# Two attentions over 2048 positions on one core: the first 1024 positions' rows fetched behind the key differences, maxima 20 steps ahead instead of 22, and another order of the lead

## The chip, the core and the metric

The kernel runs on one core of one Trainium2 chip. The metric is the device time of one execution in microseconds (us). Three executions of the kernel before are the measure; one more was taken with the hardware profiler, and all lines of a profile below come from that one.

## What is computed

Two attentions over the same x (2048 positions, width 576, 32 heads of 18 columns) are mixed by a gate. A has its own keys and values for each head; in B all heads share one set of keys and values.

```python
g = _sigmoid((x * gate_w).sum(-1, keepdims=True))
a = _A_ref(x, A_wqkv, A_wo)      # softmax(q k^T * 18**-0.5) v, 32 heads, then @ wo
b = _B_ref(x, B_wq, B_wk, B_wv, B_wo)   # the same with one k and one v for all heads
return g * a + (1 - g) * b
```

All is float32, and the softmax must subtract each row's maximum: B's queries and keys are drawn eight times as large as A's.

## The kernel before, in words

There are 64 units, one for each head: units 0 to 31 are B's, 32 to 63 are A's. A unit has 16 steps, one for each 128 keys, so there are 1024 steps, and step T belongs to unit T // 16. A step makes the scores of 128 keys with all 2048 queries in four matmuls of 512 queries (`step_scores`, L757, "s" in the strings below), ScalarE takes the exponential of each (L765), and TensorE multiplies the results with the values (L772, the digits in the strings, in quarters of 128 columns).

A row's maximum must be known before its unit's first scores. It is found ahead, by a second pass of matmuls over the same product with queries and keys in each other's place: for a block M of 128 queries, the scores with 512 keys are made at L712 and VectorE reduces them (L721, "m"). A cheaper way takes two chunks of 512 keys at once: a matmul with the *difference* of two key chunks ("x", from the tile `kdb` or `keb`), of which ScalarE keeps the positive part (L715), and a matmul with the first chunk ("y"), to which VectorE adds that part and reduces (L718). So an "x" and a "y" do the work of two "m", with one VectorE reduction in place of two, and one ScalarE operation more. In the steady strings each pair of blocks (2p, 2p+1) takes an x, a y and six m. The maxima run LEAD = 22 steps ahead of the scores (L28).

When all 16 blocks of unit u are reduced, `max_rows(u)` (L723) makes a row of them: a last reduction and a transpose on VectorE (L728, L730), a split in two halves (L246, L248; on GpSimd from unit 2 on), a DMA to DRAM (`m_d<-mh`) and two DMAs back into two rows of the unit's query tile (`qs<-m_d`), which the scores' matmul subtracts as part of its product. It is called from the loop at L1258 where a string begins at T = 16u - 6.

Before the steady loop come two stages. In the first (to some 33 us) x is loaded and split into a high and a low part, and the first two weight tiles are multiplied with it in four chunks of 512 positions (`project`, L283). The rows that come out go through DRAM, since they must change partitions: `leave_first` writes q and k rows to `kq` and the key differences to `kd`, and `back`, `back2` and `load_kd` bring them back as `ksb`, `qs` and `kdb`. All but chunk 2's go on SyncE's queue; chunk 2's writes and its two reads go on GpSimd's (`late`). The second stage is the lead (`lead_steps`, L1148, to some 79 us): its string makes the first 24 blocks' maxima with x and y for both halves of the keys (`lead_max`, L1125: 47 x and 47 y; the matmuls are L1131, the reductions L1141, the positive parts L1135), and puts between them the halves A and B of six more weight units (`half_step`, L980). Blocks are taken as (0..7, first half of the keys), (8..15, first), (0..7, second), (8..15, second), (16..23, first), (16..23, second). After the 32nd y, unit 0 is complete and `max_rows(0)` is called (L1143). The string ends with the first eight scores, between fillers ("f", L1099).

The order of all matmuls is written in strings; a small clock (`Clock`) only picks which of seven PSUM banks each one takes. In the steady loop a string covers eight steps, the last 22 steps run scores alone, two at a time, with the last output units between them (L1275). `begin(T)` (L1185) issues what is due at step T and one step of the slow normalisation, except where T % 16 == 10.

SyncE's DMAs carry eight semaphores in turn: a DMA waits until the one eight places before it has landed, beside what its data need.

Of the kernel before, what the change touches and what calls it, by code (L numbers as in the profile page):

```python
# [27 lines left out]
LEAD = 22  # L28
# [133 lines left out]
def gated_mix_kernel(ctx: ExitStack, tc: tile.TileContext, xT, wall, wv, wo, out):  # L162
# [190 lines left out]
    def back(t, i, b, x0, x1, put=dma):  # L353
        n = 64 if i < 3 else 54
        put(t[b:b + n, x0:x1], kq_d[54 * i:54 * i + n, x0:x1])

    def back2(t, i, x0, x1, put=dma):
        for b in (SB, MB):
            back(t, i, b, x0, x1, put)

    def first_back():
        load_kd(kdb, ROW_KB)
        back2(qs[0], 1, 512, 1024)
# [17 lines left out]
    with tc.tile_pool(name="xs", bufs=1, side="right") as xsp:  # L381
# [90 lines left out]
        back(ksb, 0, SB, 0, 512)  # L472
        back2(qs[0], 1, 0, 512)
# [623 lines left out]
    def keep_busy():  # L1097
# [6 lines left out]
                   for M in range(M0, M0 + 8)][:-1]}  # L1104
# [43 lines left out]
    def lead_steps(ops):  # L1148

        for op in ops.replace(" ", ""):  # L1150
# [12 lines left out]
            else:  # L1163
# [5 lines left out]
    lead_steps("ABABABABABxABxyABABxyABABxyABABxyABABxyABABxyABABxyABABxyABA"  # L1169
               "BxyABABxyABABxyABABxyABABxyABABxyABABxyABABxyABvABxyABxyABvA"  # L1170
               "BxyABxyABvABxyABxyABvABxyABxyABABxyABxyABABxyABxyABABxyABxyA"
               "BABxyABxyABABxyABxyABABxyABxyABABxyABxyABABxyABxyABABxyABxyA"
               "BABxyABxyBBxyBxyBByBsfsfsfsfsfsfmsfms")
# [11 lines left out]
    def begin(T):  # L1185

        for f in at.get(T, []) + at.get(T + 1, []):
            f()
        if slow and T % 16 != 10:
            for _ in range(2 if T > 1000 or 914 < T < 930 else 1):  # L1190
                if slow:
                    try:
                        next(slow[0])
                    except StopIteration:
                        slow.pop(0)

    out_last = out_proj(8, [P])

    def emit(ops, units=0):
        for op in ops.replace(" ", ""):  # L1200
# [7 lines left out]
            elif op in "xy":  # L1208
# [4 lines left out]
                if op == "y":  # L1213
                    step_max(*divmod(2 * pos["y"], 16), 0)
                    pos["y"] += 1
            elif op == "m":
                M, c = plain.pop(0)
                step_max(*divmod(M, 16), c)
            elif op in "AB":
# [36 lines left out]
    while pos["s"] < 4 * (NSTEP - LEAD):  # L1256
        T = pos["s"] // 4
        if (T + LEAD) % 16 == 0 and (T + LEAD) // 16 - 1 < NU:  # L1258
            max_rows((T + LEAD) // 16 - 1, nc.gpsimd if T > 16 else nc.vector)
# [12 lines left out]
    max_rows(NU - 1)  # L1272


    emit("ssssss 8 ssssssUssss 7 ssssss 8 ssssss 9 ssssssUssss 7 ssssss 9 ssssssUsssss 7 ssss 6 ssssss 3 a 6 ssssssbUcssss 6 ssssssVVVVVVVVsssssss 9 9 2", 4)  # L1275
# [38 lines left out]
```

## Time and profile before

| | |
|---|---|
| median of 3 runs | 2639.48 us (2637.72 to 2640.01) |
| the profiled execution, by its own time | 2641.33 us |
| its span, first to last instruction | 2639.5 us |
| busy in the span: PE, ACT, DVE, POOL | 99%, 93%, 91%, 36% |
| first scores of unit 0 on PE | 78.62 us |
| 33.00 to 79.00 us: PE, DVE, ACT busy | 39.34, 34.94, 34.69 us of 46.00 |
| 79.00 to 2440.00 us: PE, ACT, DVE busy | 2361.00, 2236.38, 2201.30 us of 2361.00 |
| 2580.00 to 2600.00 us: ACT busy, DVE busy | 20.00, 2.85 us of 20.00 |

PE is TensorE, ACT ScalarE, DVE VectorE, POOL GpSimd and SPq SyncE's queue, where the length of a row is the time in which DMAs are issued, not that in which they move. In a row of the timeline the first number is the start, the second the length, and the bracket is the idle time before it, with what ended it. The ends of matmuls are modelled, so a PE at 99% is not a PE without waits. 1.83 us of the execution's own time lie outside its span.

### The profile page before, as it was taken

Reading aid. Unit: us, or ns where it says so; the run is one execution under the profiler, and the core shown is the slowest. Engines: PE = TensorE matmul, PEld = TensorE weight load, DVE = VectorE, ACT = ScalarE, POOL = GpSimd, SP = SyncE. Lnnn points to the kernel's source line nnn. Section 1 sums busy time; section 2 is a strip of 40 time slices with the busy share of each in tenths; the row PEclk is TensorE's granted clock in tenths of the full one; section 3 lists DMA queues with packets and bytes.
Section 4 is the critical chain, followed back from the end, with each engine's and each line's share of the span. In section 5 each row is a group of like instructions: output and inputs, shape, how many; then the busy total and the mean of one; then the engine's idle time right before and its main releaser. Section 6 shows DMA issues by size and latency. Waiting matters only on the chain.

```text
span 2639.5 us, 67524 instructions
## 1 busy us (share of the span) xinstructions
PE 2622.6 (99%) x25446; PEld 1416.8 (54%) x25446; DVE 2391.9 (91%) x4575; ACT 2450.5 (93%) x4864; POOL 942.5 (36%) x1192
## 2 busy tenths in 40 slices
PE   8999999999999999999999999999999999999999
PEld 6545545555555554554545545545455555545665
DVE  6999999999999999999999999999999989999883
ACT  5999999999999999999999999999999999999887
POOL 3345332211045435644555355544641020012113
PEclk9999999999999999999999999999999999999999
DMA  7332322212133324332544345444442333223312
GB/s 223 90 103 86 93 78 73 88 60 61 52 112 112 95 92 115 118 92 86 147 138 137 120 123 160 131 126 133 142 137 83 112 104 88 76 85 122 114 57 92
DMA packets 186305, 280.81 MB, mean 106 GB/s; under 512 B 59876, under 2 KB 147140, under 8 KB 174535
## 3 DMA queue, kind: packets, MB, share of 16 engines
q1 hardware_dynamic: 169931, 223.68, 29.5%
q0 software_dynamic: 15168, 51.43, 5.3%
q8 instruction: 200, 3.28, 0.5%
q10 hardware_dynamic: 880, 1.39, 0.1%
q14 instruction: 126, 1.03, 0.1%
HBM read 200.74 MB, written 66.90 MB: 101 GB/s over the span
## 4 chain that ended last, share of the span: by engine, by line
PE 97%; DVE 0%; POOL 0%; ACT 0%; issue 0%; ACTq 0%; DVEq 0%
PE acc L772 38%; PE bank L712 29%; PE bank L757 18%; PE bank L980 11%; PE acc L784 1%; PE bank L960 1%; PE bank L1131 0%; POOL oacc L953 0%; PE bank L1034 0%; DVE junk L1141 0%; PE bank L339 0%; DVE oacc L955 0%; ACT tmp L952 0%; ACT xd L1135 0%; PE acc L1099 0%
## 5 line engine op out<-in xcount | busy, mean ns | idle before, releaser
L765 ACT ACTIVATE pt<-bank 128x512 f32<-128x512 f32 x4096 | 2150.4, 614 | 127.9 <-PE bank L757 71.1
L721 DVE TENSOR_REDUCE mx<-bank 128x1 f32<-128x512 f32 x3002 | 1888.3, 684 | 128.6 <-PE bank L757 63.5
L757 PE MATMUL bank<-qs,ksb 56*128 56x512 f32 x2688 | 912.2, 424 | 0.0
L712 PE MATMUL bank<-ksb,qs 54*128 54x512 f32 x2270 | 815.6, 426 | 0.0
L772 PE MATMUL acc<-pt,vb 128*19 128x256 f32 (+3 forms) x6112 | 551.5, 457 | 0.0
L712 PEld LDWEIGHTS bank<-ksb,qs 54*128 54x128 f32 x2270 | 385.5, 184 | 292.0 <-ACT pt L765 159.0
L772 PE MATMUL acc<-pt,vg 128*19 128x512 f32 (+3 forms) x5952 | 531.5, 455 | 0.0
L757 PEld LDWEIGHTS bank<-qs,ksb 56*128 56x128 f32 x2688 | 442.8, 184 | 159.0 <-DVE mx L721 66.4
L757 PE MATMUL bank<-qs,ksa 56*128 56x512 f32 x1408 | 468.1, 425 | 0.0
L712 PE MATMUL bank<-ksa,qs 54*128 54x512 f32 x1232 | 441.0, 425 | 0.0
L718 DVE CUSTOM_DVE_ANT_0 junk<-bank,xb 128x512 bf16<-128x512 f32 x500 | 342.9, 686 | 34.2 <-PE bank L757 26.6
L715 ACT ACTIVATE xb<-bank 128x512 f32<-128x512 f32 x500 | 292.5, 604 | 17.1 <-PE bank L757 7.4
L712 PEld LDWEIGHTS bank<-ksa,qs 54*128 54x128 f32 x1232 | 209.8, 184 | 142.4 <-ACT pt L765 80.6
L757 PEld LDWEIGHTS bank<-qs,ksa 56*128 56x128 f32 x1408 | 225.8, 184 | 83.8 <-DVE mx L721 33.7
L246 POOL CAST rhl<-rst 128x292 fp32r<-128x292 f32 (+2 forms) x95 | 40.0, 421 | 579.6 <-issue 343.3
L772 PEld LDWEIGHTS acc<-pt,vb 128*19 128x19 f32 x6112 | 123.2, 97 | 212.7 <-issue 182.4
L772 PEld LDWEIGHTS acc<-pt,vg 128*19 128x19 f32 x5952 | 121.6, 97 | 212.0 <-issue 185.8
L246 POOL CAST mh<-mt 128x32 fp32r<-128x32 f32 x62 | 13.0, 210 | 561.3 <-DVE mt L730 453.2
L980 PE MATMUL bank<-xr,wrh 64*128 64x292 f32 (+1 forms) x1386 | 204.1, 300 | 0.0
L980 PEld LDWEIGHTS bank<-xr,wrh 64*128 64x128 f32 x1386 | 170.0, 186 | 3.5
L712 PE MATMUL bank<-kdb,qs 54*128 54x512 f32 x372 | 161.0, 433 | 0.0
L575 POOL TENSOR_TENSOR xr<-xst,xr 128x876 fp32r<-128x876 f32 (+1 forms) x77 | 159.2, 2068 | 0.0
(175 smaller groups left out, 2441.2 us busy)
## 6 DMA issues: line engine op xcount, KB each, us to landing
qs<-qk SPq DMA_DIRECT2D x366, 144.0 KB
xst<-xT SPq DMA_DIRECT2D x66, 438.0 KB
qk<-rhl POOLq DMA_DIRECT2D x66, 292.0 KB, 4.4
ksa<-qk SPq DMA_DIRECT2D x132, 144.0 KB
xst<-xT SPq DMA_DIRECT2D x66, 146.0 KB
xst<-xT SPq DMA_DIRECT2D x132, 73.0 KB
ksb<-qk SPq DMA_DIRECT2D x60, 144.0 KB
onh<-oh POOLq DMA_DIRECT2D x32, 256.0 KB, 3.6
```

Source lines behind the costliest of these rows:

```text
L246: eng_h.tensor_copy(h, src)
L575: nc.gpsimd.tensor_tensor(x[:, 5:8, 0:n], t0, x[:, 0:3, 0:n].bitcast(F32), op=OP.subtract)
L712: nc.tensor.matmul(pm, qs[u % 3][b:b + 54, i * P:(i + 1) * P], k, start=True, stop=True)
L715: nc.scalar.activation(MX["x", u, i], pm, AF.Relu)
L718: nc.vector.tensor_tensor_reduce(junk, pm, MX.pop(("x", u, i)), 1.0, -3e38, op0=OP.add, op1=OP.max, accum_out=MX[u][:, i, c:c + 1])
L721: nc.vector.tensor_reduce(MX[u][:, i, c:c + 1], pm, axis=AX.X, op=OP.max)
L757: nc.tensor.matmul(ps, kst(u)[b:b + 56, i * P:(i + 1) * P], qs[u % 3][b:b + 56, c * 512:(c + 1) * 512], start=True, stop=True)
L765: nc.scalar.activation(pt, ps, AF.Exp, scale=SCALE)
L772: nc.tensor.matmul(acc[32 * j:32 * j + 19, a:b], v_of(u, i), PT[u, i, j][:, a:b], start=(i == 0), stop=(i == 15), skip_group_check=True)
L784: nc.tensor.matmul(acc[32 * j:32 * j + 19, 256 * half + a:256 * half + b], v_of(NU - 1, i), pt[:, x + a:x + b], start=(i == 0), stop=(i == ...
L960: nc.tensor.matmul(fp[:, 0:u.n], x, y, start=(n == 0), stop=(n == len(u.ops) - 1))
L980: nc.tensor.matmul(u.fp[op][:, 0:u.n], x[b:b + 64], y[b:b + 64], start=(n == 0), stop=(n == last))
```

## The change

Five edits go together:

1. The reads of `ksb` and `qs` for the first 512 positions, which stood ahead of chunk 1's writes on SyncE's queue, now stand behind the read of `kdb`, and the four reads of `qs` become two of 1024 positions.
2. LEAD is 20: the lead makes 22 blocks' maxima (43 x and 43 y), and the steady loop takes over the two others.
3. The lead's string begins with nine pairs of A and B instead of five ahead of the first x; the rest is spread anew. It has as many A, B, v and f as before.
4. `max_rows(u)` is called as soon as the seventh operation of the unit's last pair is emitted, no longer at the start of a string.
5. Two more steps of the old tail get a pair of blocks beside their scores, and the tail is eight scores shorter. The slow steps leave out T % 16 == 12 instead of 10.

```diff
-LEAD = 22
+LEAD = 20
...
     def first_back():
         load_kd(kdb, ROW_KB)
-        back2(qs[0], 1, 512, 1024)
+        back(ksb, 0, SB, 0, 512)
+        back2(qs[0], 1, 0, 1024)
...
         high_x(4)
-        back(ksb, 0, SB, 0, 512)
-        back2(qs[0], 1, 0, 512)
         rows = leave_first(1, F0)
...
-    lead_steps("ABABABABABxABxyABABxyABABxyABABxyABABxyABABxyABABxyABABxyABA"
+    lead_steps("ABABABABABABABABABxABxyABABxyABABxyABABxyABABxyABABxyABABxyA"
...
-        if slow and T % 16 != 10:
+        if slow and T % 16 != 12:
...
+    def formed(p):
+
+        FORMED[p] = FORMED.get(p, 0) + 1
+        if FORMED[p] == 7 and p % 8 == 7:
+            max_rows(p // 8, nc.gpsimd if p > 15 else nc.vector)
...
                     pos["y"] += 1
+                    formed(pos["y"] - 1)
             elif op == "m":
                 M, c = plain.pop(0)
                 step_max(*divmod(M, 16), c)
+                formed(M // 2)
...
-    while pos["s"] < 4 * (NSTEP - LEAD):
+    while pos["s"] < 4 * (NSTEP - LEAD - 2):
         T = pos["s"] // 4
-        if (T + LEAD) % 16 == 0 and (T + LEAD) // 16 - 1 < NU:
-            max_rows((T + LEAD) // 16 - 1, nc.gpsimd if T > 16 else nc.vector)
...
-    max_rows(NU - 1)
+    emit("msmssm 4 smsmsmsys 4")
...
-    emit("ssssss 8 ssssssUssss 7 ssssss 8 ssssss 9 ssssssUssss 7 ssssss 9 ssssssUsssss 7 ssss 6 ssssss 3 a 6 ssssssbUcssss 6 ssssssVVVVVVVVsssssss 9 9 2", 4)
+    emit("ssssssUss 7 ssssss 8 ssssss 9 ssssssUssss 7 ssssss 9 ssssssUsssss 7 ssss 6 ssssss 3 a 6 ssssssbUcssss 6 ssssssVVVVVVVVsssssss 9 9 2", 4)
```

Three places show what moved. SyncE's queue at the end of the first stage, before (`phl` are projected rows, `pdhl` the key differences; the first four writes of `kq`, chunk 0's, stand just ahead of this):

```order
L168 DMA ksb<-kq 64x512
L168 DMA qs_90<-kq 64x512 x2
L168 DMA kq<-phl 54x2x512
L168 DMA kq<-phl 54x512
L168 DMA kd<-pdhl 18x1024
L168 DMA kd<-pdhl 18x512
L168 DMA kdb<-kd 54x512
L168 DMA qs_90<-kq 64x512 x2
```

and SyncE's queue at the same place in the changed kernel:

```order
L168 DMA kq<-phl 54x2x512
L168 DMA kq<-phl 54x512
L168 DMA kd<-pdhl 18x1024
L168 DMA kd<-pdhl 18x512
L168 DMA kdb<-kd 54x512
L168 DMA ksb<-kq 64x512
L168 DMA qs_90<-kq 64x1024 x2
```

The three reads that waited for chunk 0's writes have moved from ahead of chunk 1's writes to behind `kdb`.

TensorE around the first x of the lead, before, with the engines and DMA semaphores that a matmul waits for (`kdb` marks an x, `ksb` a y, `xh` and `xl` the halves of a weight unit):

```order
L980 MATMUL bank0_476<-xh_119,wl_180 128x512
L980 MATMUL bank1_478<-xh_119,wl_180 128x512
L1131 MATMUL bank2_488<-kdb_94,qs0_90 128x512 [waits DMAHW7_49,DMAHW4_49,PE_49]
L980 MATMUL bank0_476<-xh_119,wl_180 128x512
L980 MATMUL bank1_478<-xh_119,wl_180 128x512
L1131 MATMUL bank3_494<-kdb_94,qs0_90 128x512 [waits DVE_49]
L1131 MATMUL bank4_498<-ksb_93,qs0_90 128x512 [waits DMAHW5_49,DMAHW6_49,PE_49,Activation_49]
```

and TensorE around the first x in the changed kernel, whose line numbers are one lower:

```order
L979 MATMUL bank0_474<-xl_120,wh_179 128x512
L979 MATMUL bank1_476<-xl_120,wh_179 128x512
L1130 MATMUL bank2_494<-kdb_94,qs0_90 128x512 [waits DMAHW4_49,DMAHW1_49,PE_49]
L979 MATMUL bank0_474<-xl_120,wh_179 128x512
L979 MATMUL bank1_476<-xl_120,wh_179 128x512
L1130 MATMUL bank3_500<-kdb_94,qs0_90 128x512 [waits DVE_49]
L1130 MATMUL bank4_504<-ksb_93,qs0_90 128x512 [waits DMAHW2_49,DMAHW3_49,PE_49,Activation_49]
```

The first x stands four A-B pairs later, and waits for two DMAs as before, `kdb` and a read of `qs`; the second x takes, before and now, a bank that VectorE must have read (bank3, which held the projection `project(1, 1)`).

SyncE's queue at the first rows of the steady loop, before (`m_d_73` and `qs_91` are unit 1's row of maxima, `wrst` and `xst` the weights and x of the next weight units):

```order
L168 DMA m_d_73<-mh 128x64
L168 DMA qs_91<-m_d_73 1x64x32 x2
L168 DMA wrst<-wall 128x512
L168 DMA wrst<-wall 64x128 x2
L168 DMA xst<-xT 128x3x292
L168 DMA xst<-xT 128x292
```

and the same place of SyncE's queue in the changed kernel:

```order
L168 DMA xst<-xT 64x292 x2
L168 DMA wrst<-wall 128x512
L168 DMA wrst<-wall 64x128 x2
L168 DMA m_d_73<-mh 128x64
L168 DMA qs_91<-m_d_73 1x64x32 x2
L168 DMA qs_90<-qk 18x2048 x6
```

Unit 1's row has moved behind the loads that are due at step 10. Counted in scores emitted, the row of unit u is now called for between 3 and 4.25 steps ahead of its unit's first scores, where it was 6: 3 or 3.25 steps in units 1, 8, 17, 49 and 57 to 62, 3.75 to 4.25 in all others.

More of the change, by code (lines that the diff above doesn't have):

```diff
@@ L1103, in gated_mix_kernel @@
     pairs = {"x": [(M, h) for M0, h in ((0, 0), (8, 0), (0, 1), (8, 1), (16, 0), (16, 1))
-                   for M in range(M0, M0 + 8)][:-1]}
+                   for M in range(M0, min(M0 + 8, LEAD + 2))][:-1]}
     pairs["y"] = list(pairs["x"])
@@ L1168, in gated_mix_kernel @@
     begin_units(lead_units())
-    lead_steps("ABABABABABxABxyABABxyABABxyABABxyABABxyABABxyABABxyABABxyABA"
[L1170 to L1173, printed above, removed]
+    lead_steps("ABABABABABABABABABxABxyABABxyABABxyABABxyABABxyABABxyABABxyA"
+               "BABxyABABxyABABxyABABxyABABxyABABxyABABxyABABxyABABxyABvABxy"
+               "ABABxyABvABxyABABxyABvABxyABxyABvABxyABxyABABxyABxyABABxyABx"
+               "yABABxyABxyABABxyABxyABABxyABxyABABxyABxyABABxyABxyABABxyABx"
+               "yBBxyBxyBByBsfsfsfsfsfsfmsfms")
     clk.half = HALF_MM
@@ L1197, in gated_mix_kernel @@
     out_last = out_proj(8, [P])
+    FORMED = {}
+    def formed(p):
+        FORMED[p] = FORMED.get(p, 0) + 1
+        if FORMED[p] == 7 and p % 8 == 7:
+            max_rows(p // 8, nc.gpsimd if p > 15 else nc.vector)
     def emit(ops, units=0):
```

## The prediction

> **What bounds the kernel now.** I read the page first, then the timeline of TensorE for the lead.
>
> ```profile
> span 2639.5 us, 67524 instructions
> PE 2622.6 (99%) x25446; PEld 1416.8 (54%) x25446; DVE 2391.9 (91%) x4575; ACT 2450.5 (93%) x4864; POOL 942.5 (36%) x1192
> ```
>
> Three engines are above 90% over the whole span, so the steady loop leaves little to win, and its strings are not changed. What can be won lies where TensorE stands still, and the timeline of TensorE shows that at the start of the lead (L980: weight units; L1131 with `kdb`: an x).
>
> ```profile
> 33.18 1.20 PE L980 MATMUL bank<-xh,wh 64*128 64x512 f32 x8
> 34.22 0.39 PE L980 MATMUL bank<-xh,wl 64*128 64x512 f32 x2
> 39.28 0.76 PE L1131 MATMUL bank<-kdb,qs 54*128 54x512 f32 x1 [4.67 <-issue]
> ...
> 48.62 0.39 PE L1131 MATMUL bank<-kdb,qs 54*128 54x512 f32 x1
> ...
> 49.32 0.39 PE L1131 MATMUL bank<-kdb,qs 54*128 54x512 f32 x1
> ```
>
> TensorE stops for 4.67 us ahead of the first x, which waits for `kdb`. Counting the x from 0, number 8 starts at 48.62, and the next 0.70 later: that is the pace of the string there. The stretches right after the stop, with the granted clock after the five engines' busy times:
>
> ```profile
> 39.20:44.10 4.90, 4.82 (x22) 4.13 (x24) 1.86 (x5) 2.39 (x4) 0.57 (x2) 0.50 0.66 165
> 44.10:50.00 5.90, 4.77 (x37) 3.55 (x35) 4.50 (x14) 4.63 (x9) 2.94 (x3) 0.99 0.75 234
> ```
>
> After the stop TensorE runs 4.9 us at half its clock, which costs another 2.4 us. Why `kdb` comes so late stands on SyncE's queue.
>
> ```profile
> 16.68 5.16 SPq L168 DMA_DIRECT2D kq<-phl  x4
> 29.16 0.46 SPq L168 DMA_DIRECT2D ksb<-kq  x1
> 29.67 1.24 SPq L168 DMA_DIRECT2D qs<-kq  x2
> 31.01 0.82 SPq L168 DMA_DIRECT2D kq<-phl  x2
> 31.88 1.94 SPq L168 DMA_DIRECT2D kd<-pdhl  x2
> 35.53 0.27 SPq L168 DMA_DIRECT2D kdb<-kd  x1
> ```
>
> The read of `ksb` stands from 21.84 (16.68 + 5.16) to 29.16 until chunk 0's writes have landed, and the key differences wait behind it, though VectorE has them at 26.05:
>
> ```profile
> 25.37 0.68 DVE L315 TENSOR_TENSOR pdhl<-pd,pdhl 18x512 fp32r<-18x512 f32 x1
> ```
>
> **The reads behind `kdb`.** The writes of `kd` can now be issued from 26.05 and take 1.94 us, to 28.0; the read of `kdb` follows 1.71 us after that, as it did (35.53 against 31.88 + 1.94), so at 29.7, where it was 35.53. If the writes must queue behind chunk 0's, 29.16 is the least, and 31.5 I take as the most (chunk 0's writes themselves took 7.3 us from their last issue). Behind it come `ksb` (0.46) and two reads of `qs` (1.24, now of twice the bytes), so the last is issued from 31.3 on. `kdb` needed 3.75 us from issue to use (39.28 - 35.53); with that and up to 1 us for the double size the first x may start at 35.0 to 36.0. TensorE gets there at 33.18 + 9 x 0.26 = 35.5 (eight matmuls, four pairs, took 1.04 us). So the first wait goes. What is late next is the second x: its bank was read by VectorE's last operation ahead of the joins.
>
> ```profile
> 37.19 0.69 DVE L294 TENSOR_TENSOR phl<-bank,phl 128x512 fp32r<-128x512 f32 x1 [0.28 <-ACT phl L290]
> 41.07 0.69 DVE L1141 CUSTOM_DVE_ANT_0 junk<-bank,xd 128x512 bf16<-128x512 f32 x1 [3.19 <-DMA kq<-phl]
> ```
>
> It ends at 37.88. Nothing on VectorE ahead of it moves much, so x1 stands at some 37.8, and this covers a late `kdb` too: up to 31.5 costs nothing. With 0.70 for each x, x8 would be due at 37.8 + 7 x 0.70 = 42.7.
>
> But x8 needs block 8, the first of chunk 2, which goes over GpSimd's queue and is not moved; its writes wait for VectorE at 33.82. The reads, and from the view of DMAs their time to landing:
>
> ```profile
> 38.72 1.05 POOL L168 DMA_DIRECT2D qs<-kq  x2 [2.44 <-issue]
> qs<-kq POOLq DMA_DIRECT2D x2, 128.0 KB, 6.0
> kq<-phl POOLq DMA_DIRECT2D x1, 216.0 KB, 3.8
> ```
>
> The second read is issued at 39.25 and landed at 45.3; x8 came later than that anyway (48.62), so nothing shows it in the trace of before. In the changed kernel it ends a wait. Its bounds are 43.0 (with the 3.8 us of a larger write on the same queue) and 45.3; I take 43.5, since `kdb` and two reads of `qs`, which used the DMA engines from 35.5 on, are through by then. So x8 at 43.5 in place of 48.62, and the stop ahead of it is 0.8 us, too short to make TensorE slow again (a stop of 1.13 us at 47.81 lies in the stretch at 0.99).
>
> The Trainium skill (DMA: Bandwidth & Descriptors, Anatomy of one DMA) gives a DMA of GpSimd's queue 2.0 us and its bytes at 436 GB/s, an estimate of 2.3 us for 128 KB. The row says 6.0, so the trace disagrees; by that rule block 8 would be there at 41.6, x8 at 42.7, and the sum below 0.8 us better.
>
> From x8 to the 32nd y, which completes unit 0, and on to the first scores:
>
> ```profile
> 68.42 0.69 DVE L1141 CUSTOM_DVE_ANT_0 junk<-bank,xd 128x512 bf16<-128x512 f32 x1
> ...
> 69.15 0.22 DVE L728 TENSOR_REDUCE m<-mx 128x16 f32<-128x64 f32 x1
> 69.41 0.21 DVE L730 STREAM_TRANSPOSE mt<-m 128x32 f32<-128x32 f32 x1
> ```
>
> ```profile
> 70.31 0.35 SPq L168 DMA_DIRECT2D m_d<-mh  x1
> 73.74 1.31 SPq L168 DMA_DIRECT2D qs<-m_d  x2
> ```
>
> ```profile
> 78.62 0.39 PE L757 MATMUL bank<-qs,ksb 56*128 56x512 f32 x1
> ```
>
> From x8 it is 19.8 us to that y (68.42 - 48.62). The new string has 42 pairs of A and B there, the old one 40; two of 0.23 make it 20.3, so the y is at 63.8. Behind it stood 15 more joins at 0.61 (VectorE's pace in a row, below) and the row, 10.2 us in all to the first scores; four joins fewer make 7.8. The row's own way becomes the longer: its last read is issued until 75.05, 6.6 us after the y, and lands 1.4 to 3.1 us later (3.1 if it needs `kdb`'s 3.75 from its start), 8.0 to 9.7 in all; I take 8.3, since the rows are 8 KB. So the first scores come at 63.8 + 8.3 = 72.1 instead of 78.62: **-6.5 us**, between -7.6 and -3.3.
>
> **Lead 20 and the tail.** The two blocks that leave the lead are done beside two steps that ran scores alone.
>
> ```profile
> 2574.35 31.96 ACT L765 ACTIVATE pt<-bank 128x512 f32<-128x512 f32 x65 [0.42 <-PE bank L757]
> ```
>
> ScalarE runs the tail without a gap, 31.96 us for 65, so 0.49 each, and eight scores are 3.9 us. With blocks beside them, they take nine operations of ScalarE, 4.4 us, and six reductions and a join of VectorE, 6 x 0.61 + 0.69 = 4.35 us; at most the 4.8 us of two steady steps (14.3 us for six, 139.42 to 153.72 below). **+0.7 us**, 0.5 to 0.9. Output units, scores and values are as many as before.
>
> **The rows of maxima in the loop.** The row of unit u starts 1.75 to 3 steps later than before. Unit 2, then unit 58, whose way was the longest: the last reduction, GpSimd where it was busy, the two reads, the unit's first scores.
>
> ```profile
> 139.42 0.22 DVE L728 TENSOR_REDUCE m<-mx 128x16 f32<-128x64 f32 x1
> ```
>
> ```profile
> 141.98 1.25 SPq L168 DMA_DIRECT2D qs<-m_d  x2
> ```
>
> ```profile
> 153.72 0.39 PE L757 MATMUL bank<-qs,ksb 56*128 56x512 f32 x1
> ```
>
> ```profile
> 2355.80 0.22 DVE L728 TENSOR_REDUCE m<-mx 128x16 f32<-128x64 f32 x1
> ```
>
> ```profile
> 2358.76 1.28 POOL L867 TENSOR_TENSOR ot<-ot,R 128x512 f32<-128x512 f32 x1 [10.90 <-DMA R<-r_d]
> ```
>
> ```profile
> 2362.03 1.25 SPq L168 DMA_DIRECT2D qs<-m_d  x2
> ```
>
> ```profile
> 2370.10 0.50 PE L757 MATMUL bank<-qs,ksb 56*128 56x512 f32 x1
> ```
>
> From reduction to the end of the reads' issue it is 3.8 us in unit 2 and 7.5 in unit 58; with some 1.6 to land, 5.4 and 9.1. Six steps gave 14.3 us. Of 4.25 steps, 10.1 us, 1.2 go for the last matmul and join ahead of the reduction; 8.9 remain, over 3 more than usual. Of three steps, 7.15 us, 5.95 remain: just enough. Behind a late row wait the unit's scores and everything after them on TensorE. Most of the ten units with 3 or 3.25 steps should just make it; unit 58's delay came from a normalisation step that stood ahead of it on GpSimd, and which now stands three steps ahead. **+0.3 us**, 0 to 4. The reduction and transpose themselves (0.43) now stand two steps into a string. In a steady string VectorE looks so:
>
> ```profile
> 1016.99 6.08 DVE L721 TENSOR_REDUCE mx<-bank 128x1 f32<-128x512 f32 x10
> 1023.45 2.48 DVE L721 TENSOR_REDUCE mx<-bank 128x1 f32<-128x512 f32 x4 [0.38 <-PE bank L757]
> ```
>
> Ten reductions follow each other (0.61 each), and 0.38 us of idle time behind them take up the 0.43: nothing in the sum.
>
> **The sum.** -6.5 + 0.7 + 0.3 = -5.5 us. The profiled execution's own time is 2641.33 us, 1.83 outside its span; it would become 2635.8. It stands 1.85 us above the median of the runs, 2639.48, so the forecast for that is **2634.0 us**, 0.21% less. About 0.2%, or 5.3 us, is what a measurement of this kernel tells from no change.
>
> **Rivals.** *Chunk 2 holds the lead.* If the second read on GpSimd's queue lands at 45.3 as before, x8 stops 2.6 us and the gain falls to -3.7; if TensorE then goes to half its clock, as after the stop of 4.67 us, another 2.4 are lost. For it speaks the 6.0 us row, against it the smaller traffic. 2635.8 to 2638.2, say 2636.5: no change that can be told. Chance 0.23. The Trainium skill (TensorE: Matmul & The Clock Gate, Part 1) has the clock halve after an idle window of some 3.4 us; the 0.50 after 4.67 us agrees, and by that rule a stop of 2.6 us would mostly not do it.
>
> *VectorE's row reduction reaches TensorE.* If the 0.43 us in mid-string is not taken up and a fifth of it reaches TensorE in 62 units, 5.3 us go, and the time is 2639.3: no change. Against it stand the 0.38 us, for it that strings with two units have no such gap that I saw. Chance 0.15.
>
> *The rows come late.* With three steps, 5.95 us are left for a way of 5.4. If GpSimd or SyncE's queue holds those ten rows as it held unit 58's, up to 3.2 us are lost in each. From 1.1 us each the kernel is slower by more than can be told from none; at 1.9 each it is 2634.0 + 19 = 2653, at 1.3, the likelier, 2647. Against it: nothing but unit 58 was near that, and the change clears that one. Chance 0.10.
>
> **How the numbers follow.** The forecast has 0.52 and is the one case of faster; the two that end near zero make 0.38 for no change; slower 0.10. VectorE also stood still three times in the lead, around the transposes that the new string places elsewhere:
>
> ```profile
> 56.18 0.69 DVE L1141 CUSTOM_DVE_ANT_0 junk<-bank,xd 128x512 bf16<-128x512 f32 x1 [0.59 <-PE bank L1131]
> ...
> 58.36 0.69 DVE L1141 CUSTOM_DVE_ANT_0 junk<-bank,xd 128x512 bf16<-128x512 f32 x1 [0.87 <-ACT xd L1135]
> ...
> 60.56 0.69 DVE L1141 CUSTOM_DVE_ANT_0 junk<-bank,xd 128x512 bf16<-128x512 f32 x1 [0.89 <-ACT xd L1135]
> ```
>
> If these 2.35 us shrink to nothing, with the lead at -7.6, tail 0.5 and rows 0, the time is 2630.0, the low end. The forecast's own range reaches to 2637. With the first two rivals it reaches 2639.5; beyond lie the late rows.
>
> **What would show it.** In the changed profile: `kdb` issued near 29.7; no stop of over 1 us ahead of the first x; no stretch at clock 0.50 near 40 us; x8 between 42.7 and 45.3; the first scores near 72; steady stretches of the same length; at units' first scores no new wait on `qs<-m_d`; the last 20 steps without a gap on ScalarE. It is wrong if the first scores come after 75, or if TensorE waits for the rows in the loop.

## The result and the profile after

The changed kernel took 2675.18 us (median of 4, 2671.03 to 2675.94), the kernel before 2639.74 us (median of 4, 2637.72 to 2640.36). The ratio is 1.0132, with a 95% interval of 1.0115 to 1.015: 35 us slower, where the forecast was 5.5 us faster. Ratios here and below are worked out on the executions in the fast state alone, while a median is that of all executions, a few of them slow, so that a ratio need not be the quotient of two medians. The profiled execution has a span of 2674.2 us, where it was 2639.5. Three lines of the page of the changed kernel: the span, the chain of work that ended last, and the group of score matmuls, whose last two numbers are idle time ahead of them and what ended most of it.

```profile
span 2674.2 us, 67454 instructions
...
PE 95%; DMA 2%; DVE 2%; POOL 1%; SPq 0%; issue 0%; ACT 0%; ACTq 0%; POOLq 0%; DVEq 0%
...
L756 PE MATMUL bank<-qs,ksb 56*128 56x512 f32 x2688 | 920.2, 427 | 12.7 <-DMA qs<-m_d 12.1
```

TensorE waited 12.1 us for rows of maxima, in units 0, 8 and 17, the wait that should not have come. That is a third of the loss, so the rest was sought by place. Every step has four score matmuls, so the start of number 4T is the start of step T, and the difference of two starts is the length of a string. Compared in this way, profile against profile, in us:

| place | before | after | difference |
|---|---|---|---|
| start to the first scores | 78.62 | 74.15 | -4.47 |
| steps 0 to 2, and the string from T = 2 | 3.11 + 19.58 | 4.99 + 22.00 | +4.30 |
| strings from T % 16 = 2, the other 62 together | | | +0.10 |
| strings from T = 122 and 266 (units 8 and 17 begin in them) | 18.53 + 18.55 | 26.52 + 23.53 | +12.97 |
| the other 60 strings from T % 16 = 10 | 19.46 (median) | 19.75 (median) | +19.71 |
| T = 1002 to the end | 65.73 | 67.77 | +2.04 |

The sum is +34.65 us, which is the difference of the spans.

**The lead.** SyncE's queue and the timeline of TensorE in the changed kernel (L1130 with `kdb`: an x; L756: scores), and VectorE at the row of unit 0:

```profile
28.32 0.27 SPq L168 DMA_DIRECT2D kdb<-kd  x1
28.69 0.46 SPq L168 DMA_DIRECT2D ksb<-kq  x1
29.24 1.19 SPq L168 DMA_DIRECT2D qs<-kq  x2
...
61.53 0.71 SPq L168 DMA_DIRECT2D qs<-kq  x2
64.82 0.35 SPq L168 DMA_DIRECT2D m_d<-mh  x1
70.64 1.25 SPq L168 DMA_DIRECT2D qs<-m_d  x2
```

```profile
34.41 0.47 PE L1130 MATMUL bank<-kdb,qs 54*128 54x512 f32 x1 [1.49 <-DMA qs<-kq]
35.24 0.66 PE L1130 MATMUL bank<-kdb,qs 54*128 54x512 f32 x1
...
43.80 0.47 PE L1130 MATMUL bank<-kdb,qs 54*128 54x512 f32 x1 [0.99 <-DMA qs<-kq]
...
74.15 0.76 PE L756 MATMUL bank<-qs,ksb 56*128 56x512 f32 x1 [3.56 <-DMA qs<-m_d]
```

```profile
63.15 0.69 DVE L1140 CUSTOM_DVE_ANT_0 junk<-bank,xd 128x512 bf16<-128x512 f32 x1
63.88 0.22 DVE L727 TENSOR_REDUCE m<-mx 128x16 f32<-128x64 f32 x1
```

The head comes out near its forecast: `kdb` is issued at 28.32, the first x stands at 34.41 and x8 at 43.80, the 32nd y at 63.15. The end of the lead does not. The row of unit 0 is written from 64.82, but its reads are issued only at 70.64, 5.82 us later, where it was 3.43 (70.31 to 73.74). Two reads of `qs`, those of unit 2's queries (`qs[2]`), had been issued 3.3 us ahead of the write. They stood ahead of it in the kernel before as well, but there by 6.1 us:

```profile
64.23 1.06 SPq L168 DMA_DIRECT2D qs<-kq  x2
```

TensorE stops for 3.56 us, and the windows behind the stop, with the granted clock third from the end, show a second price:

```profile
74.10:79.00 4.90, 4.85 (x19) 3.51 (x19) 1.29 (x2) 4.05 (x8) 1.21 (x2) 0.50 0.30 114
79.00:84.00 5.00, 5.00 (x21) 1.77 (x19) 2.44 (x5) 2.54 (x6) 0.00 (x0) 0.50 0.79 196
84.00:85.50 1.50, 1.50 (x12) 0.16 (x8) 1.50 (x3) 1.26 (x3) 0.00 (x0) 0.50 0.46 111
85.50:86.60 1.10, 1.10 (x8) 0.65 (x6) 0.11 (x1) 0.00 (x0) 0.38 (x1) 0.50 0.96 239
```

TensorE is busy and runs at half its clock for 12.5 us, to 86.6; the +4.30 of the table's second row stand there.

**Unit 8's row.** GpSimd in the changed kernel; VectorE's reduction for this row is at 384.06:

```profile
389.18 1.41 POOL L248 TENSOR_TENSOR vwl<-wvs,vwh 128x576 fp32r<-128x576 f32 x1
390.53 0.35 POOL L666 MEMSET vst<- 128x304 f32 x1
390.82 0.21 POOL L246 CAST mh<-mt 128x32 fp32r<-128x32 f32 x1
```

The split of the row (`mh`) waits until GpSimd has cut the weights and the first positions of the value units, whose start (`begin(122)`) is now written ahead of the row. Before, the row stood at the string's boundary, ahead of `begin(122)`. The scores of unit 8 wait 5.42 us for it, and the clock is at 0.50 from 393.8 to 400.6, which is part of the 7.99 us by which that string grew:

```profile
395.63 0.76 PE L756 MATMUL bank<-qs,ksb 56*128 56x512 f32 x1 [5.42 <-DMA qs<-m_d]
```

**One string from T % 16 = 10.** VectorE in the string from T = 394, which begins at 1054.62 in the kernel before and is 19.41 us long, and at 1076.33 in the changed one, where it is 19.70 (the "group" below is a row of reductions without a gap):

```profile
1054.61 0.22 DVE L728 TENSOR_REDUCE m<-mx 128x16 f32<-128x64 f32 x1
1054.86 0.21 DVE L730 STREAM_TRANSPOSE mt<-m 128x32 f32<-128x32 f32 x1
1055.26 0.69 DVE L718 CUSTOM_DVE_ANT_0 junk<-bank,xb 128x512 bf16<-128x512 f32 x1 [0.19 <-PE bank L757]
...
1055.88 6.07 DVE L721 TENSOR_REDUCE mx<-bank 128x1 f32<-128x512 f32 x10
1062.34 2.48 DVE L721 TENSOR_REDUCE mx<-bank 128x1 f32<-128x512 f32 x4 [0.39 <-PE bank L757]
```

```profile
1076.95 0.69 DVE L717 CUSTOM_DVE_ANT_0 junk<-bank,xb 128x512 bf16<-128x512 f32 x1 [0.67 <-PE bank L756]
...
1077.57 3.68 DVE L720 TENSOR_REDUCE mx<-bank 128x1 f32<-128x512 f32 x6
1081.28 0.22 DVE L727 TENSOR_REDUCE m<-mx 128x16 f32<-128x64 f32 x1
1081.54 0.21 DVE L729 STREAM_TRANSPOSE mt<-m 128x32 f32<-128x32 f32 x1
1081.67 2.44 DVE L720 TENSOR_REDUCE mx<-bank 128x1 f32<-128x512 f32 x4
1084.33 2.48 DVE L720 TENSOR_REDUCE mx<-bank 128x1 f32<-128x512 f32 x4 [0.22 <-PE bank L756]
```

The pair of reduction and transposition stood at the start of the string, where VectorE had to wait for TensorE anyway: without the pair it idles 0.67 us there, with it 0.19. It now stands in the row of ten reductions, which were back to back. From 1077.57 to the last group it is 6.76 us instead of 6.46. Of the 0.43 us, the gap behind the ten reductions has taken up 0.17 (0.39 became 0.22). The waits of TensorE's weight loads (total in us, times, longest) name the new holder in the changed kernel; the kernel before has no such wait on `m`:

```profile
PEld bank L711 <- DVE m L727: 13.5, 32, 0.4
```

In 32 units a weight load for a block stands until the row's reduction has let VectorE go on. This names the holder; how much of the loss it is, the experiments have to tell.

### The profile page after: what moved, and what is told of

Its sections match the earlier page's. It is cut to its first block, busy times and chain, and to the rows that moved or that the text cites. A ratio compares the mean times of both kernels' runs of the same rounds, so it can differ in the third digit from the quotient of the medians.

```text
span 2674.2 us, 67454 instructions
## 1 busy us (share of the span) xinstructions
PE 2649.2 (99%) x25446; PEld 1423.0 (53%) x25446; DVE 2392.2 (89%) x4575; ACT 2455.0 (92%) x4861; POOL 943.3 (35%) x1192
## 4 chain that ended last, share of the span: by engine, by line
PE 95%; DMA 2%; DVE 2%; POOL 1%; SPq 0%; issue 0%; ACT 0%; ACTq 0%; POOLq 0%; DVEq 0%
PE acc L771 37%; PE bank L711 28%; PE bank L756 18%; PE bank L979 11%; DVE mx L720 1%; PE bank L283 1%; PE acc L783 1%; SPq L168 0%; PE bank L959 0%; DMA m_d<-mh 0%; POOL vwl L248 0%; PE bank L1130 0%; DMA qs<-m_d 0%; DMA wst<-wall 0%; DMA kq<-phl 0%
## 5 line engine op out<-in xcount | busy, mean ns | idle before, releaser
L756 PE MATMUL bank<-qs,ksb 56*128 56x512 f32 x2688 | 920.2, 427 | 12.7 <-DMA qs<-m_d 12.1
L711 PE MATMUL bank<-ksb,qs 54*128 54x512 f32 x2277 | 831.4, 429 | 0.7 <-DVE mx L720 0.5
L756 PEld LDWEIGHTS bank<-qs,ksb 56*128 56x128 f32 x2688 | 445.2, 185 | 181.6 <-DVE mx L720 67.3
L756 PE MATMUL bank<-qs,ksa 56*128 56x512 f32 x1408 | 470.8, 425 | 0.0
L711 PEld LDWEIGHTS bank<-ksa,qs 54*128 54x128 f32 x1232 | 210.3, 184 | 144.6 <-ACT pt L764 86.6
L756 PEld LDWEIGHTS bank<-qs,ksa 56*128 56x128 f32 x1408 | 226.2, 184 | 85.9 <-DVE mx L720 32.8
```

What stands on the lines that cost most here:

```text
L711: nc.tensor.matmul(pm, qs[u % 3][b:b + 54, i * P:(i + 1) * P], k, start=True, stop=True)
L756: nc.tensor.matmul(ps, kst(u)[b:b + 56, i * P:(i + 1) * P], qs[u % 3][b:b + 56, c * 512:(c + 1) * 512], start=True, stop=True)
```

## The experiments

What each theory said, A (VectorE's time in mid-string), B (other banks), C (rows late on a queue), D (the end of the lead), stands in the expectations. Lengths are taken from the starts of scores, as in the table, against the profile of the kernel before.

**The head alone, with lead 22.** The two edits of the reads, and in the lead's string nine pairs of A and B first:

```diff
         load_kd(kdb, ROW_KB)
-        back2(qs[0], 1, 512, 1024)
+        back(ksb, 0, SB, 0, 512)
+        back2(qs[0], 1, 0, 1024)
...
-        back(ksb, 0, SB, 0, 512)
-        back2(qs[0], 1, 0, 512)
...
-    lead_steps("ABABABABABxABxyABABxyABABxyABABxyABABxyABABxyABABxyABABxyABA"
+    lead_steps("ABABABABABABABABABxABxyABABxyABABxyABABxyABABxyABABxyABABxyA"
...
```

> Kernel before (lead 22, rows of maxima at the string boundary) with two parts of the change alone: the read of ksb and the first 1024 positions of qs behind kdb, and nine pairs of A and B at the head of the lead's string (the four pairs are taken from its end, where VectorE's joins set the pace). Theory: the head's gain is real and the loss of the changed kernel lies in the loop. Then kdb is issued near 28.3 us as in the changed kernel, the 32nd y of VectorE stands near 63.2 (68.42 before), 15 joins follow, and the first scores stand near 73.4 to 74.2 (78.62 before); all strings of the loop keep their length within 0.1 us; 2634 to 2636 us. Rival: the row of unit 0, which took 11.0 us from the 32nd y in the changed kernel because its reads queued behind those of qs[2], is later than the joins (10.2 us) and TensorE stops and runs at half its clock after it: some 3 us of the gain go, 2638.

Measured: 2641.1 us against 2639.12, ratio 0.9998 (0.9981 to 1.0016). The loop keeps its length (the 62 strings from T % 16 = 10 -0.98 us together, those from T % 16 = 2 behind the first +1.83), the first scores stand at 73.58, and the rival was right about the rest:

```profile
61.64 0.97 SPq L168 DMA_DIRECT2D qs<-kq  x2
62.65 0.35 SPq L168 DMA_DIRECT2D m_d<-mh  x1
70.64 1.30 SPq L168 DMA_DIRECT2D qs<-m_d  x2
```

The row needs 8.0 us from write to read behind the reads of `qs[2]`; TensorE stops 3.29 us and is at clock 0.50 from 74.2 to 84.4, and the steps to T = 10 take 3.3 us more. Most of the head's gain is given back within its own lead.

**The row ahead of the reads of qs[2].** In addition:

```diff
-        back2(qs[2], 3, 0, S)
...
             max_rows(0, nc.vector)
+            back2(qs[2], 3, 0, S)
```

> As the kernel with the head alone, and the two reads of qs[2] are issued behind the row of unit 0 instead of ahead of it. Theory (the row's round trip grew from 3.4 to 5.8 us behind the reads of qs[2]): the row's reads are issued 3.4 us after its write, the first scores stand near 73.4 and follow the last join without a stop over 0.5 us, no stretch at half clock behind them; 2634 us. Rival (the DMA is slow there for another reason, such as the other writes of the lead): the round trip stays over 5 us and the time is that of the kernel with the head alone.

```profile
65.62 0.35 SPq L168 DMA_DIRECT2D m_d<-mh  x1
67.15 1.24 SPq L168 DMA_DIRECT2D qs<-m_d  x2
68.43 1.24 SPq L168 DMA_DIRECT2D qs<-kq  x2
```

The round trip is 1.53 us, and the first scores at 73.43 wait for no row, although x8 had stopped 2.23 us for chunk 2 in this run. One part of the expectation failed: the clock is at 0.50 from 78.1 to 81.5, with no stop ahead of it, and steps 0 to 10 take 1.15 us more than before. 2636.42 us against 2639.12, ratio 0.9982 (0.9965 to 1.0). It is the one version ahead of both kernels, by an amount at the edge of what can be told.

**A second pair in mid-string.** Kernel before, with

```diff
+        if FORMED[p] == 7 and p % 8 == 0 and p > 15:
+            clk.other(MAXED)
+            nc.vector.tensor_reduce(sr[:, 0:16], sx, axis=AX.X, op=OP.max, negate=True)
+            nc.vector.transpose(sq, sr)
```

> Kernel before with a second 64-to-16 reduction and a second 32x32 transposition (on scratch tiles, 0.43 us of VectorE, told to the bank planner as the real pair is) at the place in the string where the changed kernel has the real pair, once in each of units 2 to 63; the real pair stays at the boundary. Theory A (VectorE's 0.43 us in mid-string reach TensorE): each string that begins at T % 16 = 10 grows by about 0.3 us, 62 of them by 19 us, 2658. Rival B (the strings of the changed kernel are longer through other banks or the shifted blocks, not through VectorE's time; VectorE takes the 0.43 up in its gaps, as the prediction had it): the strings keep 19.41 us, 2640.

Measured: 2650.01 us, ratio 1.0033 (1.0015 to 1.0052). The strings from T % 16 = 10 grew by 10.26 us together, 0.17 us each (median in the middle of the loop), the others by 0.61. So B's "taken up in the gaps" falls and theory A holds in kind, but at 0.17 us instead of 0.3: only about half of the changed kernel's loss is there. From the end of the operation ahead to the start of the next this pair took 0.30 us (median over the units), the real one in the changed kernel 0.43: its reduction reads what the one ahead has just written and starts 0.03 behind it, where the scratch one starts 0.08 before the other's end.

**The planner's entry alone.** The same place in the kernel before, where only the clock that picks the banks is told of the pair (`MAXED`), with

```diff
+        if FORMED[p] == 7 and p % 8 == 0 and p > 15:
+            clk.other(MAXED)
```

> Kernel before, where only the bank planner is told of a second 0.43 us on VectorE at the place in the string where the changed kernel has the row's reduction and transposition; VectorE itself does nothing more. Theory A (what costs is VectorE's time, not the banks that the planner then chooses): strings from T % 16 = 10 keep 19.41 us within 0.05, span 2639 to 2640. Rival B (part of the 0.30 us per unit is the other choice of banks; the run with a second pair gave 0.165 of it): up to 0.14 us per string, 2648.

2638.72 us, one run; the strings gave +0.01 us (median), 1.84 together. Other banks are not the cause.

**The second pair, reading the unit's own maxima.**

```diff
-            nc.vector.tensor_reduce(sr[:, 0:16], sx, axis=AX.X, op=OP.max, negate=True)
+            nc.vector.tensor_reduce(sr[:, 0:16], MX[p // 8], axis=AX.X, op=OP.max, negate=True)
```

> As the kernel with a second pair in mid-string, but the second reduction reads the unit's own maxima, which the reduction just ahead of it has written, as the real one does. With unread scratch data the pair took 0.30 us from the end of the operation ahead to the start of the next and cost 0.165 us per unit; the real pair in the changed kernel took 0.43 and cost 0.30. Theory A2 (VectorE takes up a fixed 0.13 to 0.17 us in its gap, and the rest reaches TensorE one for one; the reduction that must wait for the one ahead adds 0.13): 0.28 to 0.30 us per unit, span 2657. Rival (the difference comes from elsewhere in the changed kernel, its blocks shifted by one pair or its DMAs): 0.165 again, 2649.

2656.37 us, one run; the strings +0.29 us (median), 16.54 together, in a kernel that has its lead, blocks and DMAs from before. In the steady strings this is the changed kernel's whole loss (+0.29); of its 19.71 us together some 3 are not reproduced, and their cause stays open. The wait on the pair stands here too:

```profile
PEld bank L715 <- DVE sr L1209: 15.6, 37, 0.4
```

The run with the unread scratch pair has the same line to the digit (15.6 us, 37 times) at 10.26 us of loss, so this wait tells who holds TensorE and not how much it costs. The lengths tell that: 0.30 us of VectorE gave 0.17 and 0.43 gave 0.29. By these two runs, 0.13 to 0.14 are taken up and the rest reaches TensorE in full.

**The row begun at once, with lead 22.** Kernel before with `formed` as in the change; the pair falls a quarter of a step ahead of the boundary.

```diff
-            max_rows((T + LEAD) // 16 - 1, nc.gpsimd if T > 16 else nc.vector)
...
+        if FORMED[p] == 7 and p % 8 == 7:
+            max_rows(p // 8, nc.gpsimd if p > 15 else nc.vector)
```

> Kernel before, lead 22, with that part of the change alone that begins a row of maxima as soon as its last pair has seven of eight operations. The row's pair then stands a quarter of a step ahead of the boundary between two strings instead of at it. Theory A3 (the place decides: VectorE idles 0.2 us at the end of a string and 0.2 to 0.6 at the start of the next, in mid-string it does not): the string that ends there grows by 0.1 us at most and the next shrinks or keeps its length, 0 to 6 us in all, 2640 to 2646. Rival (a pair at any place but the boundary costs 0.30): 2657.

2640.55 us, one run; strings from T % 16 = 10 +0.00 (median) and 0.90 together, the others 0.16. The same pair, on the same data, costs nothing there, though from the end of the operation ahead to the start of the next it takes 0.69 us (median): VectorE waits for TensorE behind it. The place decides, not the pair.

**Two pairs at the boundary.**

```diff
             max_rows((T + LEAD) // 16 - 1, nc.gpsimd if T > 16 else nc.vector)
+            clk.other(MAXED)
+            nc.vector.tensor_reduce(sr[:, 0:16], sx, axis=AX.X, op=OP.max, negate=True)
+            nc.vector.transpose(sq, sr)
```

> Kernel before with a second reduction and transposition on scratch tiles right behind the real pair, at the boundary at T % 16 = 10. There VectorE idles 0.19 us (median) behind the real pair; in mid-string the same second pair cost 0.165 us per unit. Theory A3 (the place decides): 0.05 to 0.15 us per unit, 3 to 9 us, since 0.19 of 0.30 us are free. Rival (a second pair costs the same anywhere): 10.3 us.

2641.09 us, one run; +0.01 (median), 0.40 together, the strings from T % 16 = 2 +1.32, no more than in the run with the head alone. My 0.05 to 0.15 was too much: the boundary has room for a second pair, more than the 0.19 us of idle time behind the first show.

**Rows 8 and 17 on VectorE.** The changed kernel, with

```diff
-            max_rows(p // 8, nc.gpsimd if p > 15 else nc.vector)
+            max_rows(p // 8, nc.gpsimd if p > 15 and p // 8 not in (8, 17) else nc.vector)
```

and the reads of `qs[2]` behind the row of unit 0.

> The changed kernel with two repairs at two places: rows 8 and 17 are split on VectorE instead of GpSimd, and the two reads of qs[2] are issued behind the row of unit 0. Theory C (those two rows came late because their split stood on GpSimd's queue behind the start of the next group of weight units): the strings from T = 122 and 266 fall from 26.52 and 23.53 to about 19.8 us each, -10.5 us. Theory D (the lead ends late through the queue of qs[2], and TensorE is slow after the stop): first scores at 72.1 to 72.5 instead of 74.15, and the steps behind them 4 us shorter. Together 2659 to 2661. Rival: the rows wait for SyncE's queue or the weights' DMAs; then the two strings stay over 22 us.

2662.95 us, ratio 1.0082 (1.0051 to 1.0113). Theory D: the first scores stand at 69.48, further forward than I had put them (the row's way from its reduction at 62.94 is 6.5 us), and steps 0 to 10 are as long as before, 3.10 and 19.61 us. Theory C held for unit 8 (20.15 us; the row is on time, and its split now takes 1.2 us of VectorE, 0.30 and 0.94, behind which TensorE stands for 0.71) and failed for unit 17 (24.81), where the rival was right. SyncE's queue, then GpSimd and TensorE:

```profile
753.26 1.48 SPq L168 DMA_DIRECT2D wrst<-wall  x3
754.84 0.53 SPq L168 DMA_DIRECT2D m_d<-mh  x1
756.73 1.24 SPq L168 DMA_DIRECT2D qs<-m_d  x2
```

```profile
751.63 1.60 POOL L248 TENSOR_TENSOR wrl<-wrst,wrh 128x640 fp32r<-128x640 f32 x1
```

```profile
759.50 0.76 PE L755 MATMUL bank<-qs,ksb 56*128 56x512 f32 x1 [1.98 <-DMA qs<-m_d]
```

The row's halves were ready at 751.81, but its write stood on SyncE behind a load of weights into `wrst`, which waited until GpSimd had cut the weights there (751.63 + 1.60). A queue in order passes a wait on, whichever engine prepares the row. The stop was 1.98 us, the clock 0.50 until 766.0, and the string 6.26 longer than before.

**The groups begun behind the rows.** The changed kernel, with the reads of `qs[2]` behind the row and

```diff
-    when(VA - 8, lambda: (early("vx"), begin_units(value_units())))
-    when(RB - 8, lambda: (early("px"), begin_units(row_units(RA, MT))))
+    when(VA - 4, lambda: (early("vx"), begin_units(value_units())))
+    when(RB - 4, lambda: (early("px"), begin_units(row_units(RA, MT))))
```

> The changed kernel, with the start of the value units and of the second group of weight units four steps later (T = 126 and 270 instead of 122 and 266), so that rows 8 and 17 stand ahead of them on GpSimd and on SyncE, and with the reads of qs[2] behind the row of unit 0. With rows 8 and 17 split on VectorE, row 8 was on time (string 20.15 us) but row 17 was still late (24.8 us): SyncE had its write behind a load of weights that waited for GpSimd. Theory C2 (order on both queues): both strings fall to about 19.8 us, nothing late, and of the loop's loss only the 0.30 us per unit stays, 19 us; span about 2653, time 2655 to 2657. Rival (the groups then start too late for their first units): TensorE waits for vw or wr in the strings from T = 130 or 274, and part of the gain moves there.

2655.24 us, ratio 1.0058 (1.004 to 1.0076). The two strings are 18.78 and 18.88 us (they are the shorter ones without units, so my 19.8 stood on the wrong base; it is +0.25 and +0.33 on 18.53 and 18.55). TensorE waits for no row anywhere. Against the kernel before: first scores -9.21, steps 0 to 2 0.00, strings from T % 16 = 2 +0.89, from T % 16 = 10 +20.28, tail +1.68, together +13.64. With C and D mended, what is left stands in the strings where theory A has it; the second pair that reads the unit's own maxima reproduces 16.54 of these 20.28 us.

**Strings moved by two steps.** Lead 20, but the two added steps at the start of the loop, so that the row, called at the boundary again, falls on one (T % 16 = 12). The turning points of the loop stand two steps later (not shown).

```diff
-    while pos["s"] < 4 * (NSTEP - LEAD - 2):
+    emit("msmssxm 4 smsmsmsys 4")
+    while pos["s"] < 4 * (NSTEP - LEAD):
...
+        if (T + LEAD) % 16 == 0 and (T + LEAD) // 16 - 1 < NU:
+            max_rows((T + LEAD) // 16 - 1, nc.gpsimd if T > 16 else nc.vector)
```

> Lead 20 with the head of the changed kernel and the reads of qs[2] behind the row of unit 0, but the two steps that were added at the end of the loop stand at its start, so that all strings begin at T % 16 = 4 and 12 and the row of maxima stands at the boundary again, as in the kernel before, ahead of what begins there on GpSimd and SyncE; all turning points of the loop are two steps later. If theories A, C and D are right, nothing of the loop's loss is left: strings at 19.41 us, no late row 8 or 17, first scores near 69.5 (78.62 before), and lead with tail as in the run with the two repairs, -9.1 and +2.6: span 2633, time 2634 to 2635 (ratio 0.9975 to 0.998). Rival (a lead of 20 by itself costs in the loop, since rows have two steps less on their way): unit 58 and others come late, 2640 or more.

2662.21 us, ratio 1.0091 (1.0074 to 1.0107): the expectation failed. Half of the strings kept their length; those from T % 16 = 12 grew by 0.16 us in the middle of the loop and by 1.2 to 1.6 in twelve strings (the five without units, and the seven with two units from T = 796 on), 25.1 together. For these twelve, and two more with 0.6 and 0.7, the waits of TensorE in this kernel name the cause:

```profile
PE acc L770 <- DVE oe L794: 17.1, 14, 1.5
```

The copy of `acc` at a unit's end, 0.69 us of VectorE, stood at the other boundary (T % 16 = 2) and now stands in mid-string, and the values of the next unit wait for it once in each of these 14 strings, 0.5 to 1.5 us. The strings with two units ahead of T = 260 grew by 0.3 us at most, so that the order inside the string counts and not its number of units. That the copy is also behind the 0.16 us in the middle of the loop is argued from its place, not shown. The same with the loads of queries, keys, differences and values moved too (the first of four such lines):

```diff
-        when(16 * (u - 3) + 17, lambda u=u: load_q(u))
+        when(16 * (u - 3) + 19, lambda u=u: load_q(u))
```

> Lead 20 with strings that begin at T % 16 = 4 and 12 once more, but the loads of each unit's queries, keys and values also begin two steps later, as the strings do; in the first try they stood ahead of the writes of some of those rows, so that it read rows of other contents, with the same amount of work. What was slow in the first try: every string that begins at T % 16 = 12, by 0.16 us in the middle of the loop and by 1.5 us where two units stand in a string, 25 us in all. Theory A4 (the place decides, for the other fixed work of VectorE too: the 0.69 us copy of acc at a unit's end, which stood at a boundary and now stands in mid-string): the same again, span 2658 to 2661. Rival (the early loads made it slow): strings at 19.41 us and span 2633.

2669.51 us, one run; the same strings by the same amounts (0.16, and 1.2 to 1.6 in the twelve). So the early loads are not what made them slow, and A4 stands for the strings, as far as the waits show it. The span, 2667.7, is above the 2658 to 2661 expected: the first scores stand 2.6 us later than in the first try, and a row that came 2.1 us late made one string 3.7 us longer. Neither kernel computes the two attentions rightly. Both are off by the same amount, so the early loads, which the expectation names, are not the reason; it stays open. Both issue the same instructions, group by group in the same number, as the kernel with the later starts; they are read here for the lengths of their strings alone and neither is offered as a version.

Not tried: a string whose own order leaves VectorE a gap at the place where a lead of 20 puts the row.

## Why the prediction was wrong

- **What bounds the lead, and the reads behind `kdb`**: right in the main. `kdb` 28.32 (forecast near 29.7), x8 43.80 with the wait for chunk 2 (43.5), 32nd y 63.15 (63.8). Three steps on the way were wrong. The first x waits 1.49 us, for `qs` of twice the size, where no stop over 1 us was to be. x1 follows at 35.24, not at 37.8: VectorE's operations ahead did move (L294 ended at 35.18, where it was 37.88). And the half clock that was to vanish is still there from 35.4 to 38.8; behind it the clock is 1.00, where it was 0.50 to 44.2. x8 came out right because it hung on chunk 2's reads and not on these.
- **The base.** The same head, unchanged, gives first scores at 78.62, 77.22, 73.91, 76.35, 76.74 and 76.53 in six profiles (before, and the five experiments that keep its lead). The profile I summed against was the latest of them, 2 us behind the median, so that some 2 us of the forecast gain belonged to that one execution. The -4.47 of the table, one profile against another, is no larger than this spread.
- **"the row's own way becomes the longer ... I take 8.3"**: this step failed. It took 11.0 us (63.15 to 74.15). I had carried the round trip of the kernel before (3.43 us) over as a fixed time. It was the rest of a wait behind the two large reads, which went out 6.1 us ahead of the row; now the row came 5.5 us earlier and the reads only 2.7, and it became 5.82. It is 1.53 with those reads behind it. And the stop brought half clock, 4.3 us more, which the sum did not have, though I had read that price at the head of the lead.
- **"Lead 20 and the tail", +0.7 us**: mis-sized, +2.0 (1.7 to 2.6 in the runs with that tail). Two steps with blocks take 4.60 us, within my bound of 4.8; but I set 3.9 us against them, ScalarE's pace, where the two steps before took 3.07 by the starts of their scores. These steps give 1.5 of the 2.0; where the other 0.5 stand is open.
- **"The rows of maxima in the loop", +0.3 us**: the rival had the right kind of cause. The two rows that came late belonged to the ten that I had listed with 3.25 steps or less; I argued from the row that had been slowest before (unit 58, which indeed was on time) instead of asking what is now written ahead of each row on GpSimd and SyncE. It cost 12.4 us (12.97 less twice the 0.29 of the other strings).
- **"0.38 us of idle time behind them take up the 0.43: nothing in the sum"**: the costliest failure, 20 us, and shown for some 16.5 of them by the second pairs: alone, with only its planner's entry, and at other places. Idle time of VectorE that ends on TensorE is not free room when TensorE itself is held by VectorE's banks just before. A third of the 0.43 was taken up, where the rival had said that a fifth gets through.

Term by term, the lead gave -0.2 (-4.47 + 4.30) for -6.5, the tail +2.0 for +0.7, the rows +12.4 for +0.3, the pair in mid-string +20.3 for nothing: +34.6 with what the other strings gave, where the sum was -5.5. In short, two rivals' mechanisms (VectorE and late rows) came true at once, the first four times as large as I had priced it, and a term of the forecast was lost to a queue. The forecast's own gain was real: with the row of unit 0 ahead of the large reads the first scores stand at 69.4 to 69.5, 9.2 us ahead of the profile that I summed against and 7.2 ahead of the median of the six (76.63), the blocks that went to the end included.

## What to carry to other kernels

A row of work that is free at the boundary of two strings need not be free three steps further on; test a place by putting a second copy of the work there, since an idle gap that waits for the next engine is not room if that engine was waiting for this one. When a step moves, read on every queue that it uses what now stands ahead of it, DMAs that wait for another engine above all. A lead, a string length and a unit's length belong together: with 22 steps both fixed pieces of VectorE's work, the row and the copy of `acc`, fall on boundaries of strings of eight, and no shift of the strings alone does that for 20 (12 and 2 differ by no multiple of eight).

## What the hardware showed that I had not expected

The reads of a row's maxima were issued 1.53 to 1.99 us after the row's small write in the five runs with nothing large just ahead on SyncE's queue. In the eight profiles in which the two 432 KB reads of `qs[2]` stand ahead, they came 3.43 to 7.99 us after the write, but always 8.6 to 9.5 us after the first of the large reads: the row waited for these, whenever it was written. The Trainium skill (DMA: Bandwidth & Descriptors, Queues, rings and completion order) says that the write of a DMA's semaphore lands only after every earlier write from that DMA engine, across its queues; by that rule the row must wait for the large reads, and the trace agrees. It would look the same if the row's data merely stood in the queue behind theirs; no run here tells the two apart.

The granted clock in these traces changes on a grid of 3.41 us, and between the first matmuls and the end of a run a stretch at 0.50 lasts 3.41, 6.83, 10.24 or 13.65 us, one to four windows. The four windows around unit 17's late row, in the run with rows 8 and 17 on VectorE:

```profile
755.79:759.20 3.41, 1.73 (x22) 0.65 (x19) 2.22 (x5) 2.71 (x6) 3.41 (x4) 1.00 0.10 21
759.20:762.61 3.41, 3.10 (x22) 1.16 (x22) 1.30 (x3) 1.08 (x2) 3.33 (x5) 0.50 0.54 161
762.61:766.02 3.41, 3.41 (x24) 1.74 (x26) 1.89 (x3) 1.57 (x3) 0.09 (x1) 0.50 0.69 240
766.02:769.43 3.41, 3.41 (x30) 1.22 (x28) 3.13 (x7) 3.17 (x7) 0.00 (x0) 1.00 0.06 22
```

A stop of 1.98 us lay almost whole in the first window and left TensorE busy for 1.73 us of it; the next window is at half clock. The stop of 2.23 us at x8 in the run with the row first lay across two windows, with 1.83 and 2.77 us busy, and the clock stayed at 1.00. In the thirteen traces of this case, from 28 us on, all fifteen falls behind a window with a stop follow one with at most 1.82 us busy, and no window with so little kept the clock. Two more falls have no stop: there the windows count as busy throughout, by modelled ends, but hold only 12 and 13 matmuls. The Trainium skill (TensorE: Matmul & The Clock Gate, Part 1) has the clock halve after an idle window of about 3.4 us and come back after a busy one of as much. The trace agrees with the length of the window, not with "idle": half a window of standing still was enough. Nor was any busy window enough for the return. In the changed kernel, behind the stop of 3.56 us, two windows that count as busy throughout, with 12 matmuls begun in each, stayed at 0.50, and one with 16 brought the clock back.
